# Fused attention and gated MLP on one core: new order table, a larger bias to ScalarE and edges between the first five transfers

## The chip, the cores and the metric

The kernel runs on one core of one Trainium2 chip. The metric is the device time of the program in microseconds (us). The kernel before takes 677.21 us, the median of 3 runs (676.0 to 678.33). Lower is better.

## The reference

Local attention with pooled blocks, and then a gated MLP on its output:

```python
# q, k, v: 4 batches, 8 heads, 768 rows, 64 columns; block 32, window 16
k_sum = k.reshape(B, H, nb, block, D).max(axis=3)
v_sum = v.reshape(B, H, nb, block, D).mean(axis=3)
scores_l_m = np.where(mask_l, scale * q @ k.T, -1e9)      # |row - column| < 16
scores_s = scale * (q @ k_sum.T) + np.log(block)
a = np.exp(all_scores - max); a = a / (a.sum(-1) + 1e-9)
x = (a @ np.concatenate([v, v_sum], axis=2))              # as 3072 x 512
g = x @ w_gate                                            # 512 x 1536
out = (g * sigmoid(g) * (x @ w_val)) @ w_out              # 1536 x 512
```

The three weights arrive as 8-byte numbers.

## The kernel before

**Tiles.** A unit (k,u) is half k of the rows (k = 0 to 7, two halves of 384 rows for each batch) and pair u of heads (0 to 3). For each unit, TensorE makes the scores (SC, L610 against keys kt and pooled keys ks, L617 and L623 add the mask), VectorE takes the negative maximum (nm, L663), ScalarE the exponentials p with their sums sm (L677), an engine adds the 1e-9 (eps, L700 or L702), VectorE takes the reciprocal ri (rcp, L705), VectorE or GpSimd multiplies (nrm, L708), TensorE transposes p in two groups of three blocks (PP0 and PP1, L729), ScalarE or VectorE copies them out (pt0 and pt1), and TensorE multiplies with the values (XO, L762). A multiplication by a vector of means gives the pooled values of batch 0 (FV, L787), whose results are copied through vs into the value tiles vn and vw. Then x is split into a high and a low part (xh, xl), so that each product of the MLP is three matmuls.

**The MLP.** The weights come in raw 8-byte form in tiles raw_w0 to raw_w11 and raw_o0, o2 to o10 of 1 MB, and are decoded to 4-byte numbers by five operations: abs on ScalarE (L941), clamp, shift, sign and low on VectorE (L945, L951, L958, L964), after which hi is cast and lo is a subtraction. Batch 0 multiplies plainly (g and v, L1105); batches 1 to 3 use a scheme of seven products (p, L1147) on sums of weight blocks (sumA11 and the like, and the transfers whole, sf, ss) and of x (T1 to T4, B11 and the like). A gated product a is split into hh and hl, and the accumulation with w_out (acc, L1219) gives the output.

**What sets the order.** The program's steps are recorded first, each with a name, a cost for every engine that may do it, and what it depends on. The function order (L273 to L294) computes for every step a due time, by walking the steps backwards, changes the due times by the table NUDGES (a number is an offset, a letter d, a or p fixes the engine to VectorE, ScalarE or GpSimd, s with a number is a slack for a TensorE step), and then lets run (L301 to L408) place them one by one on a planned clock: each engine takes the ready step with the earliest due time, with a penalty for waiting. Where several engines may do a step, an engine declines if another would end earlier, BIAS (L204) being added to each one's end (L373 to L374). Transfers are priced by moved (L106 to L112) and are all issued on SyncE's queue (L482). The steps are emitted in the order of their planned starts, and every engine's instructions are tied to that order. So a step that waits holds all that stands behind it on its engine.

**Fillers.** Where the plan has TensorE idle ahead of a step, before 110 us, the step is preceded by warm-up matmuls on a zero tile: int((idle - 0.5)/0.25) of them, at most 30 (L1470 and L1471; the matmuls are at L1260).

Of the kernel before, what the change touches and what calls it, by code (L numbers as in the profile page):

```python
# [214 lines left out]
fv(3) -24.8 d; PP0(0,1) s0.6; pt0(0,1) +183.2 a; pt1(0,1) -26.3; FV(0) s4.6; fv(0) +54.5 d; nrm(0,2) +49 p
PP1(0,3) s0.6; XO(0,1) s1.3432; xh(1,0) +2.1 d; val2(3) +44.5 p; XO(0,3) s1.8; xh(3,0) +0.9 d; pt1(0,0) +44.3
raw_w0 -2.8; abs_w0 +68.8; lo_w0 -39.8; wa0 +27.3; odd1(0) +180.1; val2(0) -123.8 p; odd1(2) +53 a; val1(2) +4.8 p
val2(2) +1.3 p; abs_w1 +117.3; clamp_w1 +327.1; sign_w1 -90.9; q(1,0) +61.9; SC(1,0) s3.3; scl(1,0) -76.7 d
mul(0,0) -222.6; hh(0,0,0) -10.3 d; hl(0,0,0) +67.7 d; raw_w2 +31.8; sumA22_w2 +113.7 d; sumA12_w2 -32.4 d
scl(1,1) -72.2; exp0(1,1) +31.1; pt1(1,0) -84.2 d; values(1,1) +306.9; pt0(1,1) -39.1 d; pt1(1,1) -100.1  # L220
exp5(1,3) -130.7; eps(1,3) -102.1 p; raw_o0 +33.8; clamp_o0 +68.2; shift_o0 +158.4; low_o0 +72.2; raw_o2 +66.9
hi_o2 +67.7; raw_w3 -24.5; shift_w3 -150.5; sign_w3 +11.1; sumA11_w3 +76.8 d; values(1,2) +103.5 d; PP0(1,2) s1.9
PP1(1,2) s1.1; pt1(1,2) +145.2 d; values(1,3) +10.9 a; hl(0,1,1) -22.1 p; hh(0,2,1) -9.5 a; hh(0,3,1) -144.4 d
hl(0,3,1) +196.9 d; sf4 +110.8; hl(0,4,0) +78 d; kt(1,0) +154.6; pool(1,0) +198.5; vpool(1,0) +112.7; kw(2,1) +169.5
join(2,1) -183.7 a; exp4(2,0) +66; exp4(2,1) +59.7; eps(2,1) +55.4 p; lo_w5 +24.3 d; sumA22_w5 -122.2 p
silu(5,0) +105.9; hl(0,5,0) -46.5 p; PP0(2,0) s0.4; pt0(2,1) +21.4 d; values(2,1) +11.4 p; mul(5,1) +121.6
part(0,1,1) +60.9; part(0,1,2) +100.7; join(2,2) -267.6 p; join(2,3) -100.3 p; nrm(2,2) +43.9 d; SC(2,3) s1.5
nrm(2,3) -78.4 p; part(0,1,4) +34.9; abs_w6 +76.2; lo_w6 +123 p; hl(0,6,0) +84.9 d; pt0(2,3) +58.9 d; pt1(2,3) +63.6
# [1298 lines left out]
```

## Time and profile before

| what | value |
|---|---|
| median of 3 runs | 677.21 us (676.0 to 678.33) |
| the profiled execution | 678.46 us |
| its span, first to last instruction | 676.8 us |
| TensorE busy | 662.9 us |
| VectorE busy | 498.9 us |
| ScalarE busy | 373.5 us |
| GpSimd busy | 130.7 us |
| moved by the DMA engines | 152.71 MB |

The engines are called PE (TensorE, PEld its weight loads), DVE (VectorE), ACT (ScalarE), POOL (GpSimd) and SP (SyncE). A row of a timeline gives the start in us, how long the row's instructions lasted, the engine, the line, the operation, its output and inputs without buffer numbers, the count, and in brackets how long the engine had been idle just before and what released it. A row of the waits gives the engine, what waited, what it waited for, the total in us, how many times, and the longest. A warm-up matmul is recorded as two.

### The profile page before, as it was taken

To read this page: it belongs to the slowest core of one execution; us is meant where nothing else is said; L and a number is where in the kernel's file an instruction comes from. 1 tells how busy PE (TensorE), PEld (TensorE's weight loads), DVE (VectorE), ACT (ScalarE), POOL (GpSimd) and SP (SyncE) were. 2 spreads that over 40 slices of the span, in tenths; PEclk is the share of its full clock that TensorE was granted. 3 is DMA by queue.
4 is the path that set the end of the run, shared out by engine and by line. 5 is a ranking of instruction groups with operands and counts; after the bars stand their busy time and mean duration, and the time that the engine had idled before them with its cause. 6 is when DMAs were issued, how large, how long until landed. Compare 5 with 4: busy or idle time off the path is not lost.

```text
span 676.8 us, 13318 instructions
## 1 busy us (share of the span) xinstructions
PE 662.9 (98%) x5077; PEld 611.0 (90%) x5077; DVE 498.9 (74%) x1073; ACT 373.5 (55%) x901; POOL 130.7 (19%) x141
## 2 busy tenths in 40 slices
...
GB/s 345 365 383 283 221 242 284 289 234 354 324 227 167 254 305 222 315 284 219 241 205 253 155 303 150 222 214 112 249 72 211 144 251 73 239 88 222 106 110 93
DMA packets 39681, 152.71 MB, mean 226 GB/s; under 512 B 4352, under 2 KB 8896, under 8 KB 32704
## 3 DMA queue, kind: packets, MB, share of 16 engines
q1 hardware_dynamic: 39616, 151.85, 63.3%
...
## 4 chain that ended last, share of the span: by engine, by line
PE 84%; DMA 8%; DVE 5%; SPq 1%; ACT 1%; issue 1%; POOL 0%; DVEq 0%; POOLq 0%
PE p L1147 35%; PE acc L1219 28%; PE g L1105 6%; PE v L1105 6%; DMA s<-ss 3%; PE xo L762 3%; DMA raw_o<-in_wo 3%; PE pp L729 2%; PE sc L610 2%; DMA s<-sf 1%; DMA vn<-in_vN 1%; SPq L482 1%; DVE p L708 0%; DVE nm L663 0%; DVE o L468 0%
## 5 line engine op out<-in xcount | busy, mean ns | idle before, releaser
L1219 PE MATMUL acc<-o,hh 128*128 128x512 f32 x570 | 178.0, 393 | 0.0
L1219 PEld LDWEIGHTS acc<-o,hh 128*128 128x128 f32 x570 | 105.4, 188 | 22.1 <-issue 1.3
L1147 PE MATMUL p<-xh_T,s 128*128 128x384 f32 x432 | 122.5, 338 | 0.9 <-DMA s<-ss 0.8
L1219 PE MATMUL acc<-o,hl 128*128 128x512 f32 x285 | 111.5, 391 | 0.0
L1147 PE MATMUL p<-xh_B,wa 128*128 128x384 f32 x288 | 84.9, 335 | 0.0
L1147 PEld LDWEIGHTS p<-xh_T,s 128*128 128x128 f32 x432 | 79.0, 188 | 3.2 <-DMA s<-ss 2.0
L463 ACT CAST hh<-a 128x384 fp32r<-128x384 f32 x73 | 37.5, 514 | 70.1 <-DVE a L468 67.3
L463 ACT COPY s<-p 128x384 f32<-128x384 f32 x64 | 30.7, 479 | 75.5 <-PE p L1147 75.1
L1147 PE MATMUL p<-xl_T,s 128*128 128x384 f32 x216 | 72.3, 335 | 0.0
L468 DVE TENSOR_TENSOR part<-acc,part 128x512 f32<-128x512 f32 x71 | 47.2, 684 | 27.0 <-PE acc L1219 27.0
L1219 PEld LDWEIGHTS acc<-o,hl 128*128 128x128 f32 x285 | 53.5, 188 | 11.8 <-DVE hl L468 0.3
L468 DVE TENSOR_TENSOR hl<-a,hh 128x384 fp32r<-128x384 f32 x84 | 49.3, 586 | 14.0 <-ACT hh L463 11.2
L653 ACT ACTIVATE p<-p,nm 128x120 f32<-128x120 f32 x144 | 55.1, 384 | 2.5 <-DVE nm L641 2.2
L468 DVE TENSOR_TENSOR c<-p,u 128x384 f32<-128x384 f32 x72 | 39.7, 552 | 22.7 <-PE p L1147 22.6
L1105 PE MATMUL g<-xh_B,w 128*128 128x384 f32 x192 | 53.7, 338 | 0.0
L1105 PE MATMUL v<-xh_B,w 128*128 128x384 f32 x192 | 53.4, 337 | 0.0
L1147 PEld LDWEIGHTS p<-xh_B,wa 128*128 128x128 f32 x288 | 53.0, 188 | 0.1
L1147 PE MATMUL p<-xl_B,wa 128*128 128x384 f32 x144 | 48.1, 334 | 0.0
L1147 PE MATMUL p<-xh_B,s 128*128 128x384 f32 x144 | 42.6, 336 | 1.0 <-DVE v L468 1.0
L1147 PE MATMUL p<-xh_T,wa 128*128 128x384 f32 x144 | 42.3, 334 | 0.0
L468 DVE TENSOR_TENSOR a<-c,a 128x384 f32<-128x384 f32 x65 | 36.2, 557 | 7.1 <-ACT a L1081 4.1
L1147 PEld LDWEIGHTS p<-xl_T,s 128*128 128x128 f32 x216 | 40.6, 188 | 0.3
...
## 6 DMA issues: line engine op xcount, KB each, us to landing
...
s<-ss SPq DMA_DIRECT2D x24, 1024.0 KB, 7.3
raw_w<-in_wgv SPq DMA_DIRECT2D x12, 1024.0 KB, 7.4
ss<-s SPq DMA_DIRECT2D x12, 1024.0 KB, 7.2
...
vw<-in_vW SPq DMA_DIRECT2D x28, 288.0 KB, 4.6
...
```

Source lines behind the costliest of these rows:

```text
L463: nc.scalar.copy(out, in_)
L468: vector[e].tensor_tensor(out=out, in0=a, in1=b, op=op)
L482: plan.add(name, {DMA: moved(name, nbytes)}, lambda e: nc.sync.dma_start(out(), in_()), reads, writes)
L610: nc.tensor.matmul(make(sc[h])[s * QT : (s + 1) * QT, c * KC + at : c * KC + at + x.shape[-1]], make(q)[hs, qs], x, start=not biased or c ...
L653: nc.scalar.activation(out=make(p)[:, i, :], in_=make(p)[:, i, :], func=AF.Exp, scale=-1.0, bias=make(nm)[:, i : i + 1], accum_out=make(sm ...
L729: nc.tensor.transpose(make(pp)[:KC, c * P : (c + 1) * P], make(p)[:, g * NT // 2 + c, :], make(id_sb))
L762: nc.tensor.matmul(ps[hs, qs], v, make(pt)[:, h, qs], start=True, stop=True)
L1105: nc.tensor.matmul(t[:, :TOK], a, x, start=u == order_of[0] and i == 0, stop=u == order_of[-1] and i == 2,)
L1147: nc.tensor.matmul(t[:, :TOK], a, x, start=first and kk == 0 and n == 0, stop=kk == 1 and n == 2, skip_group_check=not first,)
L1219: nc.tensor.matmul(ps[:, :wide], a, w, start=j == js[0] and m == 0, stop=j == js[-1] and m == 2)
```

## The change

It has four parts. The first five transfers, kt(0,1), vn(1), q(0,1), kt(0,3) and q(0,3), are tied to each other by edges in the plan, and vn(1) is moved right behind kt(0,1) in the list that is walked backwards. The cost of the first seven raw weight transfers in the plan is multiplied by 1.25, that of the vw transfers by 1.3. VectorE's bias goes from 0.3 to 0.5. And the whole table of nudges is replaced. What is computed stays the same; which engine does a step, and the order on each engine, change. Line numbers of the changed kernel are 20 higher than before in all that follows the table.

```diff
+EARLY_RAW = ("raw_w0", "raw_w1", "raw_w2", "raw_w3", "raw_o0", "raw_o1", "raw_o2")
+
+OPENING = ("kt(0,1)", "vn(1)", "q(0,1)", "kt(0,3)", "q(0,3)")
+
...
     if name in COLD:
         took *= 1.3
-    return took * {"ls": 1.45 if nbytes > 1e6 else 1.8}.get(kind, 1.0)
+    if name in EARLY_RAW:
+        took *= 1.25
+    return took * {"vw": 1.3, "ls": 1.45 if nbytes > 1e6 else 1.8}.get(kind, 1.0)
...
-BIAS = {DVE: .3, ACT: 0.0, POOL: 0.3}
+BIAS = {DVE: 0.5, ACT: 0.0, POOL: 0.3}
...
 NUDGES = """
-kt(0,1) -104.1; q(0,1) -74.3; vn(1) -74.9; kt(0,3) -72.8; q(0,2) +4.6; bias_sb +93.2; eps(0,1) -93.8 p; SC(0,3) s0.2
...
+kt(0,1) -81.7; q(0,1) -97.3; vn(1) -83.4; kt(0,3) -40.2; q(0,3) -116; kt(0,0) -32.5; kt(0,2) -37.9; q(0,2) -6.1
...
 def order(steps):
 
+    named = {s.name: s for s in steps}
+    for a, b in zip(OPENING, OPENING[1:]):
+        named[b].after.setdefault(named[a], False)
+    queue = [s for s in steps if s.name != OPENING[1]]
+    queue.insert(queue.index(named[OPENING[0]]) + 1, named[OPENING[1]])
     for s in steps:
         s.next = []
...
-        for s in reversed(steps):
+        for s in reversed(queue):
```

**Transfers behind the first five.** These are the rows of SyncE behind q(0,3), the fifth transfer, in the kernel before (kt are keys, q queries, vn and vw values, raw_w the raw weights of the MLP):

```order
L482 DMA vn1_119<-in_vR 32x256
L482 DMA kt_0_0_141<-in_kP 128x800
L482 DMA q_0_0_182<-in_qP 128x384
L482 DMA vn0_184<-in_vN 128x1536
L482 DMA vn0_184<-in_vR 32x256
L482 DMA kt_0_2_229<-in_kP 128x800
L482 DMA raw_w0_234<-in_wgv 128x2048
L482 DMA raw_w3_299<-in_wgv 128x2048
L482 DMA q_0_2_320<-in_qP 128x384
L482 DMA raw_w1_333<-in_wgv 128x2048
L482 DMA vw_1_0_371<-in_vW 96x768
L482 DMA vw_1_1_376<-in_vW 96x768
```

and in the kernel after:

```order
L502 DMA kt_0_0_140<-in_kP 128x800
L502 DMA kt_0_2_181<-in_kP 128x800
L502 DMA vn1_119<-in_vR 32x256
L502 DMA q_0_0_186<-in_qP 128x384
L502 DMA q_0_2_190<-in_qP 128x384
L502 DMA vn0_227<-in_vN 128x1536
L502 DMA vn0_227<-in_vR 32x256
L502 DMA raw_w0_253<-in_wgv 128x2048
L502 DMA vw_1_0_313<-in_vW 96x768
L502 DMA raw_w1_320<-in_wgv 128x2048
L502 DMA vw_1_1_343<-in_vW 96x768
L502 DMA raw_w2_363<-in_wgv 128x2048
```

q(0,2) moved from behind two raw weights to ahead of vn(0) and of all raw weights, kt(0,2) moved up, and raw_w3 left this stretch: it now stands behind raw_o0, whole0, q(1,0) and q(1,1).

**ScalarE around the decoding of raw_w1.** These are ScalarE's rows from the eps of unit (0,0) to the high part of weight 0 (w0) in the kernel before:

```order
L700 ACTIVATE sm_0_0_364<-sm_0_0_364 128x6
L463 COPY pt_0_1_414<-pp0_0_1_326 120x384
L463 COPY pt_0_1_414<-pp1_0_1_342 120x384
L463 COPY vn0_184<-vs_0_296 24x3x128
L463 COPY vw_1_0_371<-vs_0_296 24x768
L941 ACTIVATE m_w1_431<-raw_w1_333 128x1024
L463 COPY pt_0_3_442<-pp0_0_3_426 120x384
L463 COPY pt_0_3_442<-pp1_0_3_433 120x384
L463 CAST w0_462<-m_w0_338 128x1024
```

and in the kernel after:

```order
L720 ACTIVATE sm_0_0_337<-sm_0_0_337 128x6
L961 ACTIVATE m_w1_390<-raw_w1_320 128x1024
L483 COPY vs_0_263<-pv_0_371 24x128 x2
L483 COPY vn0_227<-vs_0_263 24x3x128
L483 COPY vw_1_0_313<-vs_0_263 24x768
L483 COPY vw_1_1_343<-vs_0_263 24x768
L483 CAST w0_449<-m_w0_331 128x1024
L483 COPY pt_0_3_469<-pp0_0_3_438 120x384
L691 ACTIVATE nm_0_2_443<-nm_0_2_443 128x6
```

The copies of unit (0,1)'s transposes (pt) moved ahead, the abs of raw_w1 now stands ahead of the value copies, and one copy more into vs (from VectorE) and one more into vw (from GpSimd) have come to ScalarE. Some rows further a second copy into vn (from GpSimd) and a cast to xh (from VectorE) stand ahead of the last exponentials of (0,2).

**GpSimd between the first g and the end of half 1.** These are GpSimd's rows from the eps of unit (1,1) to that of (1,3) in the kernel before (hl are low parts of a gated product, m_w sums of weight blocks):

```order
L702 TENSOR_SCALAR sm_1_1_766<-sm_1_1_766 128x6
L468 TENSOR_TENSOR hl_0_1_0_900<-a_0_1_0_795,hh_0_1_0_851 128x384
L468 TENSOR_TENSOR m_w3_667<-m_w3_667 128x256
L702 TENSOR_SCALAR sm_1_2_938<-sm_1_2_938 128x6
L468 TENSOR_TENSOR m_w3_667<-m_w3_667 128x256
L468 TENSOR_TENSOR hl_0_3_0_1075<-a_0_3_0_973,hh_0_3_0_1055 128x384
L468 TENSOR_TENSOR m_w2_530<-m_w2_530 128x256 x2
L702 TENSOR_SCALAR sm_1_3_1066<-sm_1_3_1066 128x6
```

and in the kernel after, from the sums of weight 2 on:

```order
L488 TENSOR_TENSOR m_w2_533<-m_w2_533 128x256 x2
L488 TENSOR_TENSOR hl_0_0_0_776<-a_0_0_0_668,hh_0_0_0_747 128x384
L722 TENSOR_SCALAR sm_1_1_781<-sm_1_1_781 128x6
L728 TENSOR_TENSOR p_1_1_780<-p_1_1_780,ri_1_1_812 128x720
L488 TENSOR_TENSOR m_w3_612<-m_w3_612 128x256
L722 TENSOR_SCALAR sm_1_2_949<-sm_1_2_949 128x6
L728 TENSOR_TENSOR p_1_2_948<-p_1_2_948,ri_1_2_1006 128x720
L488 TENSOR_TENSOR o2_1044<-m_o2_907,o2_1044 128x1024
L485 COPY vw_1_3_1047<-vs_0_263 24x768
L488 TENSOR_TENSOR m_w3_612<-m_w3_612 128x256
L722 TENSOR_SCALAR sm_1_3_1081<-sm_1_3_1081 128x6
```

The normalisations p of (1,1) and (1,2) and the low part o2 of raw_o2 came to GpSimd from VectorE, hl of (0,0,0) too; hl of (0,1,0) and (0,3,0) went to VectorE.

More of the change, by code (lines that the diff above doesn't have):

```diff
@@ L213 @@
 NUDGES = """
-kt(0,1) -104.1; q(0,1) -74.3; vn(1) -74.9; kt(0,3) -72.8; q(0,2) +4.6; bias_sb +93.2; eps(0,1) -93.8 p; SC(0,3) s0.2
[L215 to L228, printed above, removed]
@@ new lines @@
+PP1(0,1) s0.9671; fv(1) -37.1; max1(0,2) -107.5; exp1(0,2) +79.6; exp3(0,2) +79.8; eps(0,2) -165.7 a; pt1(0,3) +2.1
+odd1(1) -25.9 d; odd2(1) +67.8 d; val1(1) +69.2; xh(1,0) +46 a; val1(3) +63.2 p; xh(3,0) +15 d
+PP0(0,0) -0.2 s3.7442; hi_w0 +66.2; odd1(0) +236.6 p; val2(2) -106.6 p; raw_w1 +29.5; low_w1 +15.4; hi_w1 +67.7
+q(1,0) +33.6; SC(1,0) +1.9 s4; scl(1,0) -82.1 d; hh(0,0,0) -45.5 d; hl(0,0,0) +27.6 p; raw_w2 +30.3; shift_w2 -63.5
+sign_w2 +28.2; sumA12_w2 +64.6 d; vw(1,1) +9.1; max0(1,1) -257.8; nrm(1,1) -179.6 p; hl(0,1,0) +20.8 d
@@ new lines @@
+mul(2,0) +30.9; pt0(1,1) -36.1 d; exp4(1,3) -143.3; raw_o0 +13.7; low_o0 +197.3; hi_o0 +158.1; raw_o2 +30.2
+clamp_o2 +97; lo_o2 +15 p; raw_w3 +41.2; lo_w3 -102.8 d; sumA21_w3 +232.2 d; sumA11_w3 +34.7 d; sumA12_w3 +166.6
+mul(3,0) +138.4; hh(0,3,0) +120.1 d; values(1,2) +231.9 d; PP0(1,2) +2.1 s1.1; PP1(1,2) +2.1 s0.8
+part(0,0,0) +175.2 a; values(1,3) +34.4 p; hh(0,2,1) -32.9 a; hl(0,3,1) +150.6 d; lo_w4 -186.7; sumA11_w4 +13.4 d
+sf4 +245.9; abs_o4 +118.7; vt(1,0) +138.2; pool(1,0) +271.9; vpool(1,0) +141.5; kw(2,1) +592.8; ttr0(2,0) -92.6
@@ new lines @@
+exp1(2,0) +107; ttr1(2,1) +195.4; exp0(2,1) +95.9; eps(2,1) -18.6 p; low_w5 -101.9; silu(5,0) +177.2
+pt1(2,1) -100.7 d; values(2,0) +97.4 a; values(2,1) -21.8 d; hh(0,5,1) -217.3 a; part(0,1,2) +265.3; kw(2,2) +76
+join(2,2) -127 a; xf(2,1) +107.2 d; eps(2,2) -130.2; exp0(2,3) +81.1; part(0,1,3) +128.4; lo_w6 +29.9 p
+hl(0,6,0) +122.9 d; PP0(2,2) -1 s0.4; pt0(2,2) +19.9 d; pt0(2,3) +16.6; vs(1,3) +43.4; PP1(2,3) -1 s6.5
+hl(0,6,1) -92.8 p; clamp_w7 -126; shift_w7 +254.6; low_w7 -129.8; q(3,0) +35.5; XO(2,2) s0.7; ttr1(3,0) +202.3
@@ new lines @@
+exp4(3,0) +314.3; eps(3,0) +105.7 p; ttr0(3,1) +203; ttr1(3,1) +50.2; exp1(3,1) +55.8; exp4(3,1) +222.2
+hh(0,7,1) -18.3 d; clamp_w8 +128.8; shift_o8 -86.9; hi_o8 +172.1; hh(0,8,0) +19.1 a; hl(0,8,0) +92.6 p
+silu(8,1) +88.3; PP0(3,0) -1 s4.1; pt0(3,0) +264.7 a; values(3,0) -318.7 p; values(3,1) +65.7 d; part(0,2,2) -142.1
+kw(3,2) -165; join(3,2) +108.6 d; join(3,3) -62.6 p; XO(3,0) s0; vw(3,3) +51.8; exp2(3,2) +105.5; exp3(3,2) +71.4
+eps(3,2) +58.5 d; nrm(3,2) -46 p; exp3(3,3) +119.9; part(0,2,4) +36.2; abs_w9 +100.4; lo_w9 +177.8 p; sf9 -162.9
@@ new lines @@
+hh(0,9,1) +115.4 a; pt1(3,2) +71.5 d; pt1(3,3) +7 d; values(3,2) +58.3 p; values(3,3) +11.1; abs_w10 -73.6
+shift_w10 +276.6; abs_o10 +38.5; clamp_o10 +292.1; shift_o10 +414.9; hh(0,10,0) -222.5 a; XO(3,2) s3.7
+sumA12_w0 +98.9 d; raw_w11 +60.1; clamp_w11 -142.7; lo_w11 -18.8 p; T4(1,0) +82.5 d; T3(1,1) +76.6; T1(1,1) -61.3 p
+T3h(1,1) -10.5 d; T1h(1,1) +30.2 d; T4(1,1) +106.4 d; la(1,0) +256.4; mul(1,0,0) -30 p; hh(1,0,0) -109.8 a
+hh(1,0,1) +117; q(4,0) +25.9; pool(2,0) +284.2; kt(2,1) +78.5; kw(4,1) +160.7; exp4(4,0) -47.1; eps(4,0) -24.4 p
@@ new lines @@
+sumA12_w8 -85.1 p; sh(8) +81.6 d; sl(8) +13.7 p; ss(8) +44; c12(1,8) +69.3; kw(5,2) +91.8; join(5,2) -15.4 p
+q(5,3) +111.4; XO(5,0) -1.2 s2.0754; XO(5,1) -1.2 s4.2; exp1(5,2) +67.5; eps(5,2) -113.8 a; exp1(5,3) -35.8
+exp2(5,3) -155.8; sumA22_w9 +240.6 p; ss(9) +82.8; c12(1,9) -258.9; PP0(5,2) -1.2 s5.4; values(5,3) +106 p
+sh(10) -27.5 d; sl(10) -29.9 p; vv(1,10) -115.7; sumA11_w11 +8.1 p; sumA12_w11 -77.4 p; T3(2,1) +25.6 p
+mul(2,0,0) -27.6 p; mul(2,0,1) +31.1 d; kw(6,0) -218.8; kw(6,1) -45.3; join(6,1) +120.8; ttr1(6,0) +22.2
```

41 lines of the change are left out of this document (17 added, 24 removed).

## Prediction

> **What bounds the kernel now.** I read the page first, then the busy times by stretch, then TensorE's waits, then the timelines of the opening and of 50 to 75 us.
>
> ```profile
> span 676.8 us, 13318 instructions
> PE 662.9 (98%) x5077; PEld 611.0 (90%) x5077; DVE 498.9 (74%) x1073; ACT 373.5 (55%) x901; POOL 130.7 (19%) x141
> ```
>
> TensorE (PE) is busy for 662.9 of 676.8 us, and the change neither adds nor removes one of the kernel's own matmuls. All that can move is the 13.9 us in which PE stands, and the fillers. The next view splits this by stretch (columns: length, then busy time and instructions of PE, PEld, DVE, ACT, POOL, then the granted clock, the DMA share and GB/s):
>
> ```profile
> 0.00:36.00 36.00, 29.37 (x468) 26.29 (x469) 27.17 (x49) 24.19 (x77) 13.65 (x28) 1.00 0.97 358
> 36.00:75.00 39.00, 37.88 (x449) 34.45 (x448) 38.33 (x61) 31.77 (x83) 10.90 (x10) 1.00 0.82 305
> 75.00:640.00 565.00, 563.11 (x3987) 519.95 (x3986) 414.78 (x931) 308.70 (x724) 106.18 (x103) 1.00 0.63 220
> 640.00:677.00 37.00, 32.58 (x179) 30.36 (x177) 18.65 (x34) 8.82 (x18) 0.00 (x0) 1.00 0.26 93
> ```
>
> Length minus PE's busy time: 6.6 us idle in the opening, 1.1 from 36 to 75, 1.9 in the next 565, 4.4 in the tail. The granted clock is 1.00 throughout. In the opening the DMA engines are full (0.97). From 36 to 75 VectorE (DVE) has work for 38.33 of 39 us: there DVE is the engine that can make PE late. The waits of PE, by what released them:
>
> ```profile
> PE pp L1260 <- ACT pt L463: 1.9, 1, 1.9
> PE sc L610 <- DMA q<-in_qP: 1.4, 2, 0.9
> PE p L1147 <- DVE v L468: 1.0, 1, 1.0
> PE pp L729 <- ACT pt L463: 0.8, 1, 0.8
> PE pp L729 <- DVE p L708: 0.7, 1, 0.7
> ```
>
> and where the ones the change can reach lie on PE's timeline:
>
> ```profile
> 19.86 0.45 PE L610 MATMUL sc<-kt,q 64*64 64x96 f32 x5 [0.88 <-DMA q<-in_qP]
> 29.52 2.05 PE L1260 MATMUL pp<-warm 128*128 128x128 f32 x16 [1.91 <-ACT pt L463]
> 32.65 0.54 PE L729 MATMUL pp<-id_sb,p 128*120 128x128 f32 x3 [0.76 <-ACT pt L463]
> 35.28 0.44 PE L1105 MATMUL g<-xh_B,w 128*128 128x384 f32 x1
> 66.26 0.49 PE L729 MATMUL pp<-id_sb,p 128*120 128x128 f32 x3
> 70.51 0.91 PE L762 MATMUL xo<-pt,vw 120*64 120x64 f32 x22 [0.39 <-DVE pt L465]
> 73.06 0.84 PE L729 MATMUL pp<-id_sb,p 128*120 128x128 f32 x6 [0.73 <-DVE p L708]
> ```
>
> So the opening lasts until 35.28 us, where the MLP's first matmul (g) starts. Behind it PE has work without a break until 70.51 and 73.06, where DVE is late by 0.39 and 0.73 us (1.12 together). After that only 1.9 us of waits are left before the tail.
>
> **The profiled execution and the median.** It took 678.46 us, 1.66 of which lie outside its span, and 1.25 more than the median of 677.21. I sum differences against 678.46 and carry them to the median. A difference below 0.3% (2.0 us) can hardly be told from none here.
>
> **Part 1: edges between the first five transfers.** SyncE already issues these five first and in this order, so the edges cost 0. Their larger effect is on the planned times, and so on everything that is placed after them.
>
> **Part 2: the opening in its new order.** The transfers behind the fifth change places: q(0,2) goes ahead of vn(0) and raw_w0 instead of behind raw_w0 and raw_w3; raw_w3 goes behind raw_o0; vw(1,0) goes ahead of raw_w1. I price this by the rate at which the full queue delivers. These rows give sizes, and two arrivals beside the 19.86 above:
>
> ```profile
> raw_w<-in_wgv SPq DMA_DIRECT2D x12, 1024.0 KB, 7.4
> vw<-in_vW SPq DMA_DIRECT2D x28, 288.0 KB, 4.6
> q<-in_qP SPq DMA_DIRECT2D x32, 192.0 KB, 5.4
> ```
> ```profile
> 16.87 0.21 ACT L671 ACTIVATE nm<-nm 128x6 f32<-128x6 f32 x1 [0.92 <-DVE nm L663]
> 16.98 1.15 ACT L941 ACTIVATE m_w<-raw_w 128x1024 f32<-128x1024 f32 x1
> 20.20 0.26 ACT L463 COPY vs<-pv 24x128 f32<-24x128 f32 x1
> 21.60 0.51 ACT L463 COPY vn<-vs 24x384 f32<-24x384 f32 x1
> 22.02 0.82 ACT L463 COPY vw<-vs 24x768 f32<-24x768 f32 x1
> 23.94 1.15 ACT L941 ACTIVATE m_w<-raw_w 128x1024 f32<-128x1024 f32 x1 [1.10 <-DMA raw_w<-in_wgv]
> 31.06 1.16 ACT L941 ACTIVATE m_o<-raw_o 128x1024 f32<-128x1024 f32 x1 [1.60 <-DMA raw_o<-in_wo]
> 33.56 0.83 ACT L463 COPY pt<-pp 120x384 f32<-120x384 f32 x2
> 35.23 0.86 ACT L463 CAST xh_B<-xo 128x384 fp32r<-128x384 f32 x2
> ```
>
> Between q(0,2) at 19.86 and raw_o0 at 31.06 came raw_w1, two vw, raw_w2 and raw_o0 (of raw_w's shape): 3 x 1024 + 2 x 288 = 3648 KB in 11.20 us, 326 KB a us. By that, q(0,2) comes at least 2 x 1024/326 = 6.3 us earlier, so the 0.88 us wait goes; raw_w0 comes 192/326 = 0.6 later; raw_w1 (1024 - 288)/326 = 2.3 earlier; raw_o0 1024/326 = 3.1 earlier, so ScalarE's (ACT's) waits of 1.10 and 1.60 go.
>
> What sets the opening's end is ACT: the first g follows the last copy of the softmax's transposes (pt, 33.56 + 0.83 = 34.39) by 0.89 us. From 16.98 to 34.39 are 17.4 us, 2.70 of them waiting: 14.7 of work. The larger bias and the nudges put more into that same chain: a second value copy into vs (0.26), vn (0.51) and vw (0.82), a cast xh (0.86 / 2 = 0.43) and the small scaling of nm (0.21) that DVE, POOL or a later place had: 2.2 us. New end: 16.98 + 0.6 + 14.7 + 2.2 = 34.5, against 34.39. So the removed waits are paid back almost whole by the added copies. What is late next is DVE: the softmax maximum of (0,2), whose wait for q is gone, still stands behind the decoding of raw_w0. I take +0.3 for the first g. Bounds: -0.5 (raw_w0 not later, so ACT starts at 16.98) to +1.0 (ACT waits for DVE once more, as it does for 0.92 us ahead of nm at 16.87).
>
> The fillers (warm-up matmuls on L1260) go from 21 to 31, placed by planned idle time. Eight of them (16 records) took 2.05 us at 29.52, 0.26 each, so ten more are 2.6 us, in front of steps that wait for ACT anyway; they cost 0 as long as these waits are as long as planned, and belong to the upper bound.
>
> **Part 3: 36 to 75 us.** Two softmax normalisations, of (1,1) and (1,2), and the splitting subtraction of raw_o2 move from DVE to GpSimd (POOL), one hl subtraction net moves the other way:
>
> ```profile
> 16.97 0.99 DVE L708 TENSOR_TENSOR p<-p,ri 128x720 f32<-128x720 f32 x1
> 21.29 1.45 DVE L708 TENSOR_TENSOR p<-p,ri 128x720 f32<-128x720 f32 x1
> 22.66 1.52 DVE L964 SCALAR_TENSOR_TENSOR m_w<-raw_w,m_w 128x1024 int32<-128x1024 int32 x1
> 31.06 1.21 DVE L964 SCALAR_TENSOR_TENSOR m_w<-raw_w,m_w 128x1024 int32<-128x1024 int32 x1
> 52.49 0.89 DVE L708 TENSOR_TENSOR p<-p,ri 128x720 f32<-128x720 f32 x1
> 61.14 0.54 DVE L468 TENSOR_TENSOR hl<-a,hh 128x384 fp32r<-128x384 f32 x1
> 63.84 0.90 DVE L708 TENSOR_TENSOR p<-p,ri 128x720 f32<-128x720 f32 x1
> 66.47 1.21 DVE L468 TENSOR_TENSOR o<-m_o,o 128x1024 fp32r<-128x1024 f32 x1
> ```
> ```profile
> 22.05 2.51 POOL L465 COPY vw<-vn 64x384 f32<-64x384 f32 x2
> 29.47 1.39 POOL L708 TENSOR_TENSOR p<-p,ri 128x720 f32<-128x720 f32 x1 [3.90 <-DVE ri L705]
> ```
>
> DVE loses 0.89 + 0.90 + 1.21 = 3.0 and gains 0.5: 2.5 us of relief. But DVE's operations are longer beside POOL's: the two that lie beside the POOL copies at 22.05 took 1.45 against 0.99 and 1.52 against 1.21, so 0.3 to 0.46 more each. Three more POOL operations, the last about 1.39 x 1024/720 = 2.0 long and so beside two of DVE's, touch four: 4 x 0.4 = 1.6 us back. 0.9 us of relief is left against 1.12 us of waits. DVE's list also has the key maximum of (1,1) ahead of the last normalisation, which waits for its transfer. I take -0.7; bounds -1.12 (all gone) and +1.6 (below).
>
> [...]
>
> **Part 4: after 75 us.** PE's order is nearly the same, but two more pairs of transposes are torn apart: two groups of three cost 2 x 0.49 against 0.84 for six, 0.14 each, +0.3. The 1.0 us wait for v (DVE) stays, because DVE's list still has the cast that waits for a transfer ahead of it. Tail: the same instructions, 0.
>
> Sum: 0 + 0.3 - 0.7 + 0.3 = -0.1, so 678.4 for an execution like the profiled one, and 677.1 as a median.
>
> **Rivals.**
> *Faster, 22%.* ACT's chain starts at 16.98 and nothing in it waits: g 0.5 earlier. DVE's relief removes all of 1.12. The transfer behind the 1.0 us wait for v comes earlier, as its place in the order allows, and that wait goes too. -0.5 - 1.12 - 1.0 = -2.6: 674.6. For it: every load of the opening except raw_w0 and vn(0) lands earlier. Against it: 2.2 us of copies added on ACT.
>
> *Slower, 23%: POOL holds DVE.* The place is 36 to 75 us. POOL's extra work is 2 x 1.39 + 2.0 less one hl (1.39 x 384/720 = 0.7): 4.1 us. If DVE stands for all of it, DVE is not 2.5 us earlier but 4.1 - 2.5 = 1.6 later, and PE's waits at 70 and 73 us grow by that. With g at +1.0 and +0.3 for the transposes: +2.9, 680.1. It decides for "slower" once DVE is over 0.7 us later with g at +1.0. For it: DVE's share of 38.33 in 39 us, which leaves it no slack. Against it: the 0.3 to 0.46 us measured per pair. [...]
>
> *Nothing happens, 17%.* The edges name an order that stands already, the reordered work sits in ACT's and DVE's gaps, and g starts at 35.3: 677.2.
>
> **How the numbers follow.** My forecast has 38%, 2 of them below -2.0 us. Faster 22 + 2 = 24%, same 36 + 17 = 53%, slower 23%. The likeliest case gives 677.1; by itself it spans 675.9 to 678.5: -1.3 (g -0.5, -1.12, +0.3) to +1.3 (g +1.0, the waits of 1.12 as they are, +0.3). The range reaches to the two outer rivals, 674.5 to 679.8, just past the one and just short of the other; about 2 in 10 lie beyond.
>
> **What would show it.** Right: the first g between 35.0 and 36.3 us; no wait of ACT for raw_w or raw_o between 17 and 34; POOL at 13 to 16 us busy from 36 to 75; PE's waits there under 0.7 us; the 1.0 us wait for v still there. Wrong: a first g before 34.5 or after 36.5; a new wait of PE over 1 us after 75 us; normalisations on POOL that take over 2 us, with PE waiting for them.

## The result, and the profile after

The changed kernel takes 684.46 us (median of 4 runs, 682.68 to 685.82) against 676.94 for the kernel before (4 runs); the ratio is 1.0108, with a 95% interval of 1.0078 to 1.0137. It is slower by 7.5 us, where 677.1 was forecast and 679.8 was the upper end. The profiled execution took 685.82 us, 2.12 of them outside its span; 7.36 more than the profiled execution before, 6.9 of them inside the span.

The first lines of the page of the kernel after:

```profile
span 683.7 us, 13372 instructions
PE 668.6 (98%) x5097; PEld 616.4 (90%) x5097; DVE 494.2 (72%) x1048; ACT 380.8 (56%) x911; POOL 146.5 (21%) x160
```

TensorE is busy 5.7 us longer, with 20 more recorded matmuls (ten warm-ups). Ten warm-ups at 0.26 us each are 2.6 of it; the rest is the same work at a slower pace. The busy times by stretch show where (the column behind POOL's is the granted clock):

```profile
0.00:36.00 36.00, 30.80 (x424) 28.24 (x425) 25.20 (x45) 23.18 (x75) 9.18 (x27) 0.91 0.91 329
36.00:75.00 39.00, 38.09 (x475) 34.87 (x473) 36.31 (x55) 31.47 (x83) 13.09 (x12) 1.00 0.92 311
75.00:640.00 565.00, 560.11 (x3990) 516.68 (x3991) 411.96 (x913) 317.36 (x737) 124.27 (x121) 1.00 0.64 222
640.00:685.00 45.00, 39.56 (x213) 36.64 (x211) 20.70 (x37) 8.83 (x18) 0.00 (x0) 0.99 0.22 76
```

The clock of the opening is 0.91 where it was 1.00, and from 75 to 640 us TensorE stands 4.9 us instead of 1.9. Finer, around 30 us:

```profile
24.00:28.50 4.50, 1.56 (x29) 1.08 (x26) 3.79 (x7) 4.40 (x8) 2.80 (x4) 1.00 0.99 393
28.50:29.00 0.50, 0.34 (x2) 0.29 (x2) 0.50 (x1) 0.50 (x4) 0.00 (x0) 0.55 1.00 327
29.00:35.00 6.00, 6.00 (x44) 5.75 (x43) 5.67 (x10) 5.41 (x18) 0.00 (x0) 0.50 0.68 270
35.00:35.50 0.50, 0.50 (x5) 0.50 (x4) 0.50 (x2) 0.00 (x0) 0.00 (x0) 0.62 1.03 393
```

From 24.0 to 28.5 us TensorE works for 1.56 of 4.5 us. Then the granted clock falls to 0.50 and stays there for 6.8 us (from about 28.55 to 35.38, by the means of the two half-microseconds at its ends). The kernel before was busy 2.97 us in the same 4.5 and its clock stayed at 1.00. TensorE's timeline, at the places that answer to those shown of before:

```profile
25.75 0.34 PE L782 MATMUL xo<-pt,vn 120*64 120x64 f32 x4 [1.52 <-ACT vn L483]
28.66 0.84 PE L782 MATMUL xo<-pt,vn 120*64 120x64 f32 x3 [1.58 <-ACT pt L483]
30.61 4.64 PE L1280 MATMUL pp<-warm 128*128 128x128 f32 x20
39.20 0.45 PE L1125 MATMUL g<-xh_B,w 128*128 128x384 f32 x1
75.28 0.91 PE L782 MATMUL xo<-pt,vw 120*64 120x64 f32 x22 [1.07 <-DVE pt L485]
77.83 0.84 PE L749 MATMUL pp<-id_sb,p 128*120 128x128 f32 x6 [0.75 <-ACT part L483]
172.76 0.73 PE L1239 MATMUL acc<-o,hh 128*128 128x512 f32 x2 [1.57 <-ACT a L1101]
178.54 0.73 PE L1239 MATMUL acc<-o,hh 128*128 128x512 f32 x2 [0.72 <-DVE part L488]
528.21 0.44 PE L1167 MATMUL p<-xh_B,s 128*128 128x384 f32 x1 [1.28 <-DVE v L488]
```

The sum of the 6.9 us: the first g comes at 39.20 instead of 35.28, +3.9; the waits between 70 and 80 us are 1.93 instead of 1.12, +0.8; two new waits at 172 to 178 us, +2.3; the wait for v at 236.7 us is gone (-1.0) and another stands at 528 us (+1.3); the waits for weight sums (s) late in the span shrink by 0.7. That is 6.6; the rest, 0.3, is of the size that the prediction gave to the transposes torn apart, which no run here tests.

ScalarE in the opening, the rows behind the first two waits above (the last row is the copy of (0,2)'s transposes, which before ended at 34.39):

```profile
18.53 1.15 ACT L961 ACTIVATE m_w<-raw_w 128x1024 f32<-128x1024 f32 x1 [2.45 <-DMA raw_w<-in_wgv]
23.43 1.17 ACT L961 ACTIVATE m_w<-raw_w 128x1024 f32<-128x1024 f32 x1 [0.85 <-DMA raw_w<-in_wgv]
25.18 0.51 ACT L483 COPY vn<-vs 24x384 f32<-24x384 f32 x1
35.74 0.86 ACT L483 COPY pt<-pp 120x384 f32<-120x384 f32 x2 [1.25 <-PE pp L749]
37.43 0.87 ACT L483 COPY pt<-pp 120x384 f32<-120x384 f32 x2
```

The abs of raw_w1 waits until 23.43 for its transfer, and the value copies stand behind it, so vn is there only at 25.7: that is XO(0,1)'s wait.

From 23.43 on ScalarE works without a wait until 34.5, so what follows hangs on the landing of raw_w1. That landing differs between executions: in the kernels below that keep this list of transfers it is at 22.3 to 25.3 us. Two executions are therefore compared by the distance from raw_w1's abs to the first g, here 39.20 - 23.43 = 15.77 us, and not by the time of the first g alone.

### The profile page after: what moved, and what is told of

Its sections match the earlier page's. It is cut to its first block, busy times and chain, and to the rows that moved or that the text cites. A ratio compares the mean times of both kernels' runs of the same rounds, so it can differ in the third digit from the quotient of the medians.

```text
span 683.7 us, 13372 instructions
## 1 busy us (share of the span) xinstructions
PE 668.6 (98%) x5097; PEld 616.4 (90%) x5097; DVE 494.2 (72%) x1048; ACT 380.8 (56%) x911; POOL 146.5 (21%) x160
## 4 chain that ended last, share of the span: by engine, by line
PE 82%; DVE 9%; DMA 6%; issue 1%; ACT 1%; SPq 0%; DVEq 0%
PE p L1167 36%; PE acc L1239 27%; PE g L1125 5%; PE v L1125 5%; PE xo L782 3%; PE sc L630 3%; PE pp L749 3%; DMA s<-ss 2%; DMA kt<-in_kP 2%; DMA raw_w<-in_wgv 2%; PE pp L1280 1%; DVE m_o L984 1%; DVE w L488 1%; DVE m_w L978 1%; DVE m_o L978 1%
## 5 line engine op out<-in xcount | busy, mean ns | idle before, releaser
L483 ACT CAST hh<-a 128x384 fp32r<-128x384 f32 x79 | 40.4, 513 | 56.8 <-DVE a L488 52.5
L488 DVE TENSOR_TENSOR hl<-a,hh 128x384 fp32r<-128x384 f32 x81 | 47.1, 583 | 17.7 <-ACT hh L483 15.1
L661 DVE CUSTOM_DVE_ANT_0 p<-sc,bias_sb 128x120 f32<-128x120 f32 x144 | 30.7, 276 | 16.4 <-PE sc L630 16.4
L1101 ACT ACTIVATE a<-p 128x384 f32<-128x384 f32 x36 | 17.7, 492 | 41.8 <-PE p L1167 40.2
```

Of the source, the lines that this page charges most:

```text
L483: nc.scalar.copy(out, in_)
L488: vector[e].tensor_tensor(out=out, in0=a, in1=b, op=op)
L661: nc.vector.tensor_tensor_reduce(out=make(p)[:, i, :], in0=make(sc[g])[:, c * KC : (c + 1) * KC], in1=make(bias_sb)[:, 0 if n == 0 else 2 ...
L1101: name, {ACT: 0.49}, lambda e: nc.scalar.activation(out=make(a), in_=src(), func=AF.Silu), reads, (a,), table="silu"
```

## The experiments

Edits of the kernel after change only the emitted list: a step is moved to just ahead of another or to another engine, or TensorE is given a number of warm-ups ahead of a named step. Everything else keeps its order and engine. The first edit of a kind shows the form; the others only their table. Times are medians; ratios are against the kernel before on the same chip. Each profile is one execution. Labels such as e1 are those that the recorded expectations use.

**The parts one by one.** Three kernels apply one part each to the kernel before.

```diff
-BIAS = {DVE: .3, ACT: 0.0, POOL: 0.3}
+BIAS = {DVE: 0.5, ACT: 0.0, POOL: 0.3}
```

> The kernel before with VectorE's bias at 0.5 alone (old nudges, no edges, old costs). Theory 'table': the new nudges carry the loss, the bias by itself costs little: 677 +/- 2. Rival 'bias': the bias puts copies on ScalarE and GpSimd in the opening and beside VectorE's work, and carries at least half of the loss: 680.5 or more.

691.44 us, ratio 1.0222 (1.0204 to 1.024): slower than the whole change, and on the side of the rival "bias".

```diff
+EARLY_RAW = ("raw_w0", "raw_w1", "raw_w2", "raw_w3", "raw_o0", "raw_o1", "raw_o2")
+OPENING = ("kt(0,1)", "vn(1)", "q(0,1)", "kt(0,3)", "q(0,3)")
...
-    return took * {"ls": 1.45 if nbytes > 1e6 else 1.8}.get(kind, 1.0)
+    if name in EARLY_RAW:
+        took *= 1.25
+    return took * {"vw": 1.3, "ls": 1.45 if nbytes > 1e6 else 1.8}.get(kind, 1.0)
...
```

> The kernel before with the edges between the first five transfers, the raw weights charged a quarter more and the vw transfers 1.3 times, old bias and old nudges. Theory 'table': 677 +/- 2, the first five transfers already stood in this order. Rival 'edges': the planned times behind them are off and carry at least half of the loss: 680.5 or more.

682.15 us, ratio 1.007 (1.0043 to 1.0096): on the side of the rival "edges".

```diff
 NUDGES = """
-kt(0,1) -104.1; q(0,1) -74.3; vn(1) -74.9; kt(0,3) -72.8; q(0,2) +4.6; bias_sb +93.2; eps(0,1) -93.8 p; SC(0,3) s0.2
...
+kt(0,1) -81.7; q(0,1) -97.3; vn(1) -83.4; kt(0,3) -40.2; q(0,3) -116; kt(0,0) -32.5; kt(0,2) -37.9; q(0,2) -6.1
...
```

> The kernel before with the new table of nudges alone, old bias, no edges, old costs. Theory 'table': the loss of 7.5 us is here: 682 to 687. Rival 'only together': each part disturbs an order that fits the others, so this one is off as well, but by another amount and at other places than the kernel after: new waits elsewhere, over 687, or under 680.

708.95 us, ratio 1.0476 (1.0447 to 1.0505). Each part alone is slower, by 14, 5 and 32 us, together they are slower by 7.5. The parts do not add up, and the change as a whole is less bad than the table without its bias and edges. "Only together" is the theory that stands; that the table's offsets fit the bookkeeping that they were made for is read from it. No two of the parts were run together, so which pair belongs together stays open. The kernel with the edges alone is worth a look of its own:

```profile
73.06 0.91 PE L773 MATMUL xo<-pt,vw 120*64 120x64 f32 x22 [1.36 <-DVE pt L476]
75.77 0.80 PE L1230 MATMUL acc<-o,hh 128*128 128x512 f32 x1 [1.37 <-DVE o L479]
```

Its first g came at 33.61, 1.7 us earlier than before, but its clock fell to 0.50 from 30.4 to 37.2, and again from 74.8 to 81.6, at these two waits.

**The clock.** First on the kernel before, whose fillers at 29.5 us are taken away:

```diff
         if s.engine == PE and s.start < 110.0:
             spare[0] = min(30, max(0, int((s.idle - 0.5) / 0.25)))
+            spare[0] = {'PP0(0,2)': 0}.get(s.name, spare[0])
```

> The kernel before without the eight warm-up matmuls ahead of PP0(0,2) at 29.5 us; nothing else is changed. TensorE then stands from 27.6 to 31.4 us. Theory 'clock gate': that is as much standing as in the kernel after, so the granted clock falls to 0.50 at about 31 us and stays there until TensorE has been busy for some 7 us: the first g runs at half clock, +2 to +3.5 us. Rival: the clock stays at 1.00 and the time is the same, since the fillers fill only waiting: 677 +/- 1.

```profile
27.00:31.50 4.50, 0.54 (x4) 0.30 (x3) 4.50 (x9) 3.08 (x13) 1.39 (x1) 1.00 1.00 401
31.50:32.00 0.50, 0.10 (x1) 0.00 (x0) 0.50 (x1) 0.50 (x2) 0.00 (x0) 0.66 1.14 462
32.00:38.00 6.00, 5.72 (x58) 5.27 (x59) 4.38 (x7) 5.09 (x8) 0.00 (x0) 0.50 1.03 422
38.00:38.50 0.50, 0.50 (x3) 0.50 (x2) 0.50 (x2) 0.00 (x0) 0.00 (x0) 0.52 0.95 401
```

The clock falls where it did not before, for 6.8 us, and the first g (at 35.86) runs at half speed. The price is smaller than expected: 678.44 us over 10 runs, ratio 1.0019 (1.0007 to 1.0031), 1.3 us. The fillers of the kernel before earn that much.

Then the kernel after, with the two gaps filled (e1):

```diff
+            spare[0] = {'XO(0,1)': 5, 'XO(0,3)': 7}.get(s.name, spare[0])
```

> The kernel after, with more warm-up matmuls in the two places of the opening where TensorE stands: 5 ahead of XO(0,1), 7 ahead of XO(0,3) (1 before); the order of everything else is kept. Theory 'clock': TensorE stood 3.7 of the 4.6 us from 24.2 to 28.7, the granted clock then fell to 0.50 until 35.4, and this is what made the first g 3.9 us late. Filled, the clock stays at 1.00, the first g comes at 36.5 or earlier (39.2 in the kernel after) and the time falls by 2.5 us or more. Rival 'ScalarE': the first g is late because ScalarE's chain to the last transposes' copies (pt of (0,2), end 38.3) is late, and the clock only lengthens the ten fillers ahead of PP0(0,0). Then the clock stays at 1.00, ScalarE's wait of 1.25 for these transposes goes, but the first g comes at 37.9 to 38.2 and the time falls by only 1.0 to 1.3 us.

```profile
24.00:28.50 4.50, 4.10 (x57) 3.51 (x57) 4.12 (x7) 4.45 (x10) 3.13 (x4) 1.00 1.01 388
28.50:36.00 7.50, 6.27 (x86) 5.85 (x82) 7.12 (x13) 7.43 (x21) 0.00 (x0) 1.00 0.82 305
```
```profile
22.47 1.20 ACT L961 ACTIVATE m_w<-raw_w 128x1024 f32<-128x1024 f32 x1 [0.49 <-DMA raw_w<-in_wgv]
33.48 0.86 ACT L483 COPY pt<-pp 120x384 f32<-120x384 f32 x2
36.93 0.44 PE L1125 MATMUL g<-xh_B,w 128*128 128x384 f32 x1
```

The clock stays at 1.00 and the first g comes at 36.93 instead of 39.20; 681.9 us, ratio 1.0075 (1.0061 to 1.0088). But raw_w1 landed 0.96 us earlier in this execution. Counted from it, the first g comes after 14.46 us instead of 15.77: 1.3 us are the clock's. ScalarE's rows say the same: its copies of the transposes come 11.01 us behind raw_w1's abs and no longer wait, against 12.31 with the wait of 1.25. Three more kernels with these fillers (f1, f2 and g2 below) give 14.44, 14.47 and 14.46. So the size is that of the rival "ScalarE", 1.0 to 1.3 us, and 1.6 us against the kernel before are left at full clock in this execution. The time alone would not show it, since the two intervals overlap. (From 24.2 to 28.7 us TensorE of the kernel after stood 3.1 of 4.5 us by the trace, not 3.7 of 4.6 as the expectation has it.)

The opposite test, without the ten fillers ahead of PP0(0,0):

```diff
+            spare[0] = {'PP0(0,0)': 0}.get(s.name, spare[0])
```

> The kernel after without the ten fillers ahead of PP0(0,0), which took 4.6 us at half clock; all else is kept. Theory 'clock gate': the fillers are what brings the clock back; without them TensorE stands for another 3 us, the clock is still at 0.50 when the first g starts, and the time is 0.5 to 2 us longer than the kernel after. Rival 'toll': the fillers stand in the way of the transposes, without them ScalarE's wait of 1.25 us goes and the first g comes at 38 or earlier: 1 us or more is gained.

```profile
29.50:30.00 0.50, 0.00 (x0) 0.00 (x0) 0.32 (x1) 0.50 (x2) 0.50 (x1) 0.93 0.96 355
30.00:40.00 10.00, 8.18 (x72) 7.27 (x74) 9.41 (x13) 8.80 (x26) 0.18 (x1) 0.50 0.84 293
40.00:40.50 0.50, 0.50 (x21) 0.50 (x19) 0.00 (x0) 0.45 (x1) 0.00 (x0) 0.83 0.99 393
```

The clock now stays down for 10.2 us and the first g comes at 40.77; 685.75 us, ratio 1.0127 (1.011 to 1.0145), which cannot be told from the kernel after (1.0078 to 1.0137). In this execution the first scores started at 8.60 instead of 6.92 us and raw_w1 landed at 25.25; counted from it the first g comes after 15.52 us, 0.25 earlier than with the fillers. So with the fillers the fall of the clock was shorter, 6.8 us against 10.2, but neither theory is borne out: they neither gained nor cost more than 0.3 us at the first g.

**ScalarE's and VectorE's chains in the opening.** What holds the 1.6 us? First the value copies, put ahead of the abs that waits, without the fillers (pairs are "this step to just ahead of that one"):

```diff
+    for x, y in [('fv(1)', 'abs w1'), ('fv(0)', 'abs w1'), ('val2(1)', 'abs w1')]:
+        line.remove(at[x])
+        line.insert(line.index(at[y]), at[x])
```

> The kernel after, with the two copies into vs and the first copy into vn placed ahead of the abs of raw_w1 on ScalarE, instead of behind it; nothing else is moved. In the kernel after they stand behind an abs that waits until 23.4 us for its transfer. Theory 'ScalarE': XO(0,1)'s wait of 1.5 us for vn goes, ScalarE's wait for raw_w1 (0.85) is filled by the copies, so its chain ends 0.85 us earlier; with 1.5 us less standing the clock may stay at 1.00, which gives 1.2 us more: first g at 37.2 (clock 1.00) or 38.3 (clock falls again), time 0.9 to 2.0 us lower. Rival 'clock': first g at 36.5 or earlier if the clock stays, unchanged if it falls.

```profile
27.54 0.75 PE L782 MATMUL xo<-pt,vn 120*64 120x64 f32 x3 [2.50 <-ACT pt L483]
```

XO(0,1)'s wait went, and XO(0,3)'s grew from 1.58 to 2.50. The clock fell again, for 3.4 us only, and the first g came at 36.75. The abs no longer waited, so the landing of raw_w1 is not seen, and how much of the 2.45 us is the copies', the shorter fall's or the landing's this run alone does not say. 683.18 us, ratio 1.0087 (1.0074 to 1.01), whose interval overlaps that of the kernel after. Next the three steps that had come to ScalarE, back on their engines (f2, on top of the fillers and of two edits below, which lie behind the opening):

```diff
+    for x, e in (("values(1,1)", POOL), ("val2(0)", POOL), ("xh(1,0)", DVE)):
+        at[x].engine = e
```

> The kernel before this one (fillers, activation, raw_o10), with three steps of the opening put back on the engines that had them in the kernel before: the value copy into vw(1,1) and the second copy into vn(0) on GpSimd, the cast xh(1,0) on VectorE (0.82 + 0.51 + 0.43 = 1.8 us off ScalarE). Theory 'ScalarE': the 1.6 us by which the first g is still late with the clock at 1.00 (36.9 against 35.3) is this added work; g comes at 35.1 to 35.6 and the time falls by 1.3 to 1.8 us. Rival 'transfers': ScalarE starts late since raw_w0 arrives late, and waits for what is saved: g at 36.5 or later, less than 0.5 us gained.

First g at 37.39, 14.47 us behind raw_w1, where it was; 683.3 us, ratio 1.0087 (1.0074 to 1.01). The rival's times came, but not for the rival's reason: ScalarE got its 1.8 us back, but VectorE got the cast (0.54) and lost another 0.9 us, as its rows beside GpSimd's show:

```profile
24.47 2.00 POOL L485 COPY vw<-vs 24x768 f32<-24x768 f32 x2 [8.17 <-ACT vs L483]
28.00 1.39 POOL L485 COPY vw<-vs 24x384 f32<-24x384 f32 x1
```
```profile
24.78 1.33 DVE L965 TENSOR_SCALAR m_w<-m_w 128x1024 f32<-128x1024 f32 x1
27.50 1.52 DVE L488 TENSOR_TENSOR w<-m_w,w 128x1024 fp32r<-128x1024 f32 x1
29.41 1.51 DVE L978 SCALAR_TENSOR_TENSOR m_w<-raw_w,m_w 128x1024 int32<-128x1024 int32 x1
```

They took 1.00, 1.23 and 1.22 with the fillers alone. And VectorE's normalisation of (0,2), which TensorE waited 1.23 us for there and 1.17 here, is as late as ScalarE. So that one was moved up (g1):

```diff
+    for x, y in [('eps(0,2)', 'abs o0'), ('nrm(0,2)', 'clamp o0')]:
```

> The kernel after with the fillers of e1, the eps of unit (0,2) ahead of the abs of raw_o0 on ScalarE, and the normalisation of (0,2) ahead of the clamp of raw_o0 on VectorE. Theory 'normalisation': with the clock at 1.00 the first g is held by this chain, eps (at 32.3 us behind the abs), reciprocal (32.6), clamp, normalisation (33.3 to 34.1), transposes, since TensorE's one wait there is 1.23 us for it; it moves up by 0.9 to 1.2 us and so do the transposes and the first g: 35.8 to 36.1 instead of 36.9, the time falls by 0.6 to 1.2 against the fillers alone. Rival 'ScalarE': the copies of the transposes and of raw_w1's high part wait for ScalarE, whose list is full; g stays within 0.3 us.

TensorE's wait for it fell from 1.23 to 0.32, a wait of 0.41 for ScalarE's pt appeared, and the first g came at 37.51, 14.58 us behind raw_w1; 683.22 us, ratio 1.0104 (1.0088 to 1.0119). These two edits, each for one of the two engines, moved nothing. Both engines at once (h1):

```diff
+    for x, y in [('eps(0,2)', 'abs o0'), ('nrm(0,2)', 'clamp o0'), ('hi w1', 'shift w2')]:
```

> The kernel of g1_norm (fillers, normalisation of (0,2) moved up), and the cast to the high part of raw_w1 (1.06 us) on ScalarE placed behind the copies of (0,2)'s transposes instead of ahead of them. Theory 'two chains': with the clock at 1.00 ScalarE's and VectorE's lists end within half a microsecond of each other, so that relieving one alone moved nothing (first g 36.9, 37.4, 37.5 in the kernels with fillers, counted from a first score at 7.0 to 7.4); with both relieved the first g comes at 36.0 to 36.6 and the time falls by 0.7 to 1.0 against g1_norm. Rival: a third chain (TensorE's own fillers and transposes) holds it: g at 37.0 or later.

```profile
35.98 0.44 PE L1125 MATMUL g<-xh_B,w 128*128 128x384 f32 x1
```

First g at 35.98, 1.5 us earlier than in g1 and 0.7 later than in the kernel before. The abs of raw_w1 started at 22.34 here and at 22.93 in g1, so 0.9 of the 1.5 are the edit's: 13.64 us behind raw_w1 instead of 14.58. A second kernel with this edit (h2 below), whose abs waited for raw_w1, gives 13.64 too. So two chains of about equal length held half of the 1.6 us. The time, 682.56 us, ratio 1.0085 (1.0072 to 1.0098), does not show it: by their profiles, this kernel stands longer than the one with the fillers alone between 36 and 640 us (5.6 us against 4.2).

**The stretch at 172 us.** ScalarE changed its table of functions four times between 165 and 173 us in the kernel after, by loads of 1.28 us each. One edit (e3) saves two of these loads:

```diff
+    for x, y in [('silu(8,1)', 'exp1(3,1)')]:
```

> The kernel after, with the second activation of weight block 8 (silu(8,1)) placed right behind the first one on ScalarE, ahead of the exponentials of unit (3,1) that stood between them; this saves two loads of the activation table (1.28 us each). Theory 'tables': ScalarE is late at 172 us because it changes tables four times between 165 and 173; the two waits of TensorE, 1.57 us at 172.8 and 0.72 at 178.5, go, and the time falls by 1.6 to 2.3 us. Rival 'port': VectorE is late there because operations of GpSimd hold it (2.78 us for a clamp that takes 0.68), so the low part of the product stays late, the waits move but keep their size: 0 to 0.5 us.

```profile
175.61 0.72 PE L1239 MATMUL acc<-o,hh 128*128 128x512 f32 x2 [1.97 <-DVE part L488]
```

683.6 us, ratio 1.0092 (1.0073 to 1.0112). The wait for ScalarE is gone and the same 2.3 us stand at VectorE's part (1.97) and GpSimd's hl (0.34) instead: "tables" fell. The opening of this kernel is that of the kernel after, and its profile is a second sample of it: the clock fell for 3.4 us instead of 6.8, and the first g came 14.42 us behind raw_w1, as with the gaps filled. So a fall of 3.4 us cost the first g nothing here, where one of 6.8 cost 1.3. VectorE's rows there in the kernel after, and GpSimd's beside them:

```profile
159.30 2.78 DVE L965 TENSOR_SCALAR m_w<-m_w 128x1024 f32<-128x1024 f32 x1
173.12 1.76 DVE L984 SCALAR_TENSOR_TENSOR m_o<-raw_o,m_o 128x1024 int32<-128x1024 int32 x1
175.78 0.97 DVE L488 TENSOR_TENSOR hl<-a,hh 128x384 fp32r<-128x384 f32 x1
```
```profile
159.13 2.40 POOL L488 TENSOR_TENSOR w<-m_w,w 128x1024 fp32r<-128x1024 f32 x1 [2.29 <-ACT w L483]
172.08 4.26 POOL L488 TENSOR_TENSOR m_again<-m_again 128x256 f32<-128x256 f32 x3
```

Two ways to relieve VectorE, on top of the fillers and that edit. Its own work that nobody needs yet, behind the additions (f1):

```diff
+    for x, y in [('low o10', 'clamp w11'), ('hi o10', 'clamp w11'), ('lo o10', 'clamp w11')]:
```

> The kernel after with the fillers of e1, the second activation of block 8 behind the first, and the last two steps of decoding raw_o10 on VectorE (low, 2.03 us there, and lo, 1.75) with the cast between them on ScalarE placed behind the three additions to the outputs (part) at 175 us instead of ahead of them. Theory 'VectorE': the waits at 172 to 178 us come from these 3.8 us of decoding that nobody needs yet, and the activation alone only moved them; both go, 2.0 to 2.3 us less than with the fillers alone: 679.6 to 680. Rival 'port': GpSimd's operations hold whatever VectorE does there, at least 1.2 us of waits stay: 680.8 or more.

682.95 us, ratio 1.0082 (1.0066 to 1.0097). The 2.3 us fell to 0.27 between 170 and 180, and 0.86 and 0.43 came back between 180 and 190, for part and for a copy. And GpSimd's sums, behind the additions (g2):

```diff
+    for x, y in [('sumA22 w0', 'clamp w11'), ('sumA21 w0', 'clamp w11'), ('sumA11 w0', 'clamp w11')]:
```

> The kernel after with the fillers of e1, the second activation of block 8 behind the first, and GpSimd's three sums of weight 0 (m_again, 3.6 us there) placed behind the additions to the outputs at 175 us. Theory 'port': beside them VectorE's operations took 1.75 us instead of 1.21 and 0.98 instead of 0.54; without them VectorE is 0.9 us earlier or more, and the waits at 170 to 178 us fall from 2.3 to 1.4 us or less. Rival 'VectorE': its own list is too long there, whatever GpSimd does: the waits stay at 2.0 us or more.

```profile
171.96 0.56 DVE L488 TENSOR_TENSOR hl<-a,hh 128x384 fp32r<-128x384 f32 x1
172.43 1.22 DVE L488 TENSOR_TENSOR o<-m_o,o 128x1024 fp32r<-128x1024 f32 x1
174.31 0.72 PE L1239 MATMUL acc<-o,hh 128*128 128x512 f32 x2 [1.00 <-DVE part L488]
```

The two operations took 0.56 and 1.22 us instead of 0.98 and 1.75 with the activation alone, and the waits fell from 2.3 to 1.3 (1.00 here and 0.30 for hl). So about 1 us is GpSimd's toll and the rest VectorE's own list. 681.45 us, ratio 1.0073 (1.006 to 1.0087): by its time alone it cannot be told from the fillers alone.

**Sums.** The fillers, the value copies and the activation together; then all edits of the opening and of this stretch but the cast; then the fillers, both chains, the activation and GpSimd's sums:

> The three edits together: the fillers, the value copies ahead of the abs of raw_w1, and the second activation behind the first. If they add up by theories 'ScalarE' and 'tables': 2.0 + 2.0 = 4.0 us less than the kernel after, about 680.5, still 3.5 above the kernel before. If 'clock' holds: 2.5 + 0.9 + 2.0 = 5.4 or more, 679 or below.

684.21 us, ratio 1.0103 (1.0089 to 1.0118). In the profiled execution the first scores waited 1.56 us for q(0,1), 1.3 more than in the kernel after, and the 2.3 us at 172 were whole. Counted from raw_w1 (24.94) its first g came after 13.47 us, 1.0 less than with the fillers alone: the value copies ahead of the abs are worth that, and the late start hides it.

> All edits of this series on the kernel after: fillers, the normalisation of (0,2) moved up, the second activation of block 8, raw_o10's last decoding steps behind the additions, the three sums behind them too. If the causes are the ones named and add up, the opening gives 1 us and the stretch from 170 to 190 us 1.5 us against the fillers alone (681.9): 679 to 680, still 2 us above the kernel before. If each move only hands its wait to the next step: 681 or more.

683.37 us, ratio 1.0097 (1.0083 to 1.0111): each move handed its wait on, 0.9 us between 180 and 190 and 1.0 for sums, with 1.3 us of waiting for q(0,1) in its profile.

> The edits of h1_cast and of g2_sums together. If they add up: the opening 1 us and the stretch at 170 us 1 us better than the fillers alone (681.9): 679.5 to 680.5. If the stretches after them give it back: 681 or more.

680.98 us, ratio 1.0071 (1.0058 to 1.0083): the lowest of the mended kernels, 0.7% above the kernel before. By its time it cannot be told from e1 or g2, but all its runs (680.25 to 682.45) lie below those of the kernel after (682.68 to 685.82). Last, the kernel with the edges alone, filled, with one copy on another engine:

```diff
+    for x, e in (("pt1(1,2)", ACT),):
+        at[x].engine = e
...
+            spare[0] = {'PP1(0,0)': 6, 'XO(1,2)': 9}.get(s.name, spare[0])
```

> The kernel before with the edges and the changed transfer costs alone (682.15), whose first g came at 33.6 us but with the clock at 0.50 from 30.4 to 37.2 and from 74.7 to 81.9. Added: six fillers ahead of PP1(0,0), nine ahead of XO(1,2), and the copy pt1(1,2) on ScalarE instead of VectorE, which was late with it by 1.36 us. If the two falls of the clock and that wait carry its loss: clock 1.00 throughout, 675 to 678, near or below the kernel before. If its loss is elsewhere (the decoding of raw_o2 on VectorE, late by 1.37 at 75.8 us, and what follows): 679 to 681.

679.46 us, ratio 1.003 (1.0019 to 1.0041), against 682.15 without: the clock stays at 1.00 through the opening and at 75 us, the first g comes at 32.59, 2.7 us before that of the kernel before, and waits for o of 2.1 us in all (1.6 of them for VectorE) remain between 63 and 74 us. That is the second forecast's 679 to 681. The fillers and the copy were changed together, so their shares are not known. No version beat the kernel before.

## Why the prediction was wrong, point by point

**Part 1, edges at 0.** The five transfers do keep their order, but "0" hid what the edges and costs do to the plan: with the old table they cost 5 us.

**Part 2, the first g at +0.3: this is the step that failed.** It came at +3.9. Three of its terms were off. The transfers: raw_w0 was there at 18.53 instead of 17.6, raw_w1 at 23.43 instead of 21.7 (a vw and raw_w1, 1312 KB, took 4.90 us, 268 KB a us and not 326; in seven other executions of this list whose first scores had started by 7.8 us raw_w1 was there at 22.3 to 23.0), so a wait of 0.85 was left where 0 was forecast. The waits of TensorE: with the end of ScalarE's chain alone summed, the two waits of 1.52 and 1.58 us on the way, for vn and pt, were not seen; the abs of raw_w1 ahead of the value copies stood in the quoted order. And the clock: the forecast read 1.00 in every stretch and kept it. At half clock the ten more fillers took 4.64 us, and ScalarE stood 1.25 us for the transposes behind them. Of the 3.9 us, 1.3 are the clock's (15.77 against 14.46 us behind raw_w1, with the gaps filled), 1.0 goes with raw_w1's landing (23.43 against 22.47 in that run), 0.8 are the two chains' (14.46 to 13.64 with both relieved), and 0.8 are left. With Part 2 right the forecast would still have been 3.4 us low: Part 3 missed 1.5 and Part 4 1.9.

**Part 3, -0.7.** It was +0.8. VectorE's relief did not reach TensorE: the waits at 75 and 78 us are for pt on VectorE, which had itself waited for a transfer (vt, 1.34 us), and for part on ScalarE.

**Part 4, +0.3.** It was about +2.2: the 2.3 us at 172 to 178, less 1.0 at 236.7, with 1.3 at 528, less 0.7 of waits for weight sums, and 0.3. The torn transposes may be right, but "nearly the same" order of TensorE was taken for the same time. On the other engines, decoding raw_o10, GpSimd's sums and table changes had come ahead of what TensorE needs at 172 us. The wait for v at 236.7 us, said to stay, went; a similar one came at 528, behind the operands of batch 3 on VectorE.

**The rivals.** "Slower: POOL holds DVE" had the sign, 23%, but not the cause in its place: the waits there grew by 0.8 us of its 1.6, and behind a transfer and ScalarE (Part 3). VectorE's operations did take longer beside GpSimd's at 159 to 176 us, and by more than the 0.3 to 0.46 us that the forecast took: a clamp of 0.68 us took 2.78 beside an operation of 2.40. That is 2.10 us more, nearly the whole of GpSimd's operation, where the rows quoted in the prediction showed 0.31 and 0.46 beside copies of 1.25. The clock was not among the rivals; alone it would have given 1.3 of the 7 us, so no single rival would have been right.

**What stays open.** More than half of the loss in time: h2 is still 4.4 us above the kernel before on its chip, of which the two profiles show 0.85 at the first g and 0.8 of waits from 36 to 640 us. And where the clock falls in executions without a profile. In six runs of the kernel with the activation moved (its opening is that of the kernel after) the mean clock of the span and the time go together in the main, from 1.000 with 681.10 us through 0.996 with 683.91 to 0.991 with 686.29 (0.994 with 683.30 is out of line). In the kernel before the mean clock varies too, 0.995 to 1.000, with no such relation (675.82 at 0.995, 678.34 at 0.999); where it fell in those runs no trace shows. A fall can also lie behind the last matmul: in the kernel with the normalisation moved the clock stood at 0.50 for the last 2.2 us, and the last matmul had ended 2.0 us before that.
